# Retention into an ELU feed-forward, one core: the first batch's scores, masks and state copies in another order, output copies written in a row, w_out in 4 KB pieces

## The chip, the cores and the metric

One core of a Trainium2 chip runs the whole kernel. The metric is the device time of one execution in microseconds (us); for the kernel before it is the median of three runs. The engines are PE (TensorE; PEld is its weight load), DVE (VectorE), ACT (ScalarE), POOL (GpSimd) and SP (SyncE), which here only issues transfers. PSUM is the memory that PE writes its products to and that DVE and ACT read; SBUF is the main memory on the core. PSUM is used in banks of 2 KB a partition.

## The reference

Retention without a softmax over 8 batches, 8 heads, 576 positions and 64 values a head, and behind it a feed-forward with ELU:

```python
scores = scale * np.matmul(q, k.transpose(0, 1, 3, 2))         # 8 x 8 x 576 x 576
gamma = 1.0 - 2.0 ** (-5.0 - np.arange(H))                     # one decay a head
Dmat = np.where(rel >= 0, gamma[:, None, None] ** rel, 0.0)    # rel = query position - key position
ret = np.matmul(scores * Dmat, v)                              # 8 x 8 x 576 x 64
x = ret.transpose(0, 2, 1, 3).reshape(4608, 512)
h = x @ w_in                                                   # 512 x 2048
g = np.where(h > 0.0, h, np.exp(np.minimum(h, 0.0)) - 1.0)
out = g @ w_out                                                # 2048 x 512
```

## The kernel before

The decay is folded into queries and keys when they are cast to bf16 (`cast_*`, a product with a small table on DVE or POOL), so scores only need a 0/1 mask. Attention goes by units of 256 positions and 4 heads: a batch has the units (T, w), T the half of 512 positions and w the half of the heads, so units 0 to 3 are batch 0, units 4 to 7 batch 1. (From batch 3 on there are finer units of 128 positions and all heads; the last 64 positions of each batch ride along with other units.)

For each unit the steps are these. Queries and keys are turned on PE and copied from PSUM by ACT or DVE (`turn_q0`, `turn_k0`, `turn_pe`), later by a DMA transpose (`turn`). `scores` writes the products into the one score tile `sc`; `masks` (DVE) multiplies them into `pt` and so frees `sc`. `state` (`states` in the first batch) makes the sums of keys with values. `prefix_mid` and `prefix_end` add them up at the unit's middle and end, on DVE or by an ACT copy, and `put_mid` and `put_end` copy these sums into the tile `s_pair`, on POOL (or into `s_last`, which only the riders of the last 64 positions read). `outputs` takes the two output banks (`new_x`, tiles `x`), does `inter` (queries with the state in `s_pair`) and `values` (`pt` with the values), and `put_x` copies both banks into the bf16 tile `xt`, which the feed-forward reads. A copy of unit 0 to 3 writes elements at steps of four, one of unit 4 to 11 at steps of two, since the positions lie in groups: a partition of q, k or v holds 4 (or 2) positions that lie side by side in memory.

The feed-forward's first product has 16 tiles of 128 features, `ph`: 4 products of 512 columns each (`ffn1`), or for a half of the tokens two tiles of 256 columns (`ffn1_half`). `elu` runs Exp and Relu on ACT and joins them on DVE into `g`. The second product (`ffn2`) adds 16 tiles into `pm`, and ACT copies it out. For group 0, `row(ft)` is the second product's part of one feature tile for two 128-token tiles, and `behind` says after which first-product tile it comes.

Weights come as fp32 through the same staging tiles as q and k (`load_w`, 16 pieces of 512 KB, each in two transfers), and POOL casts most of them (`cast_w`): pieces 0 to 7 are w_in, 8 to 15 w_out. `warm(n)` puts 2n dummy products on PE.

The order on each engine is the order in which the code is written (`pin`, keep_in_program_order). Each engine works through its queue strictly in that order and waits where an input or a buffer isn't ready. Tiles with one tag share a fixed number of buffers: `ph` three banks, `sc` one pair of banks, `x0` and `x1` one bank each, `pt` two, `rv` five.

Of the kernel before, what the change touches and what calls it, by code (L numbers as in the profile page):

```python
# [9 lines left out]
FP32 = mybir.dt.float32  # L10
# [7 lines left out]
def kernel(  # L18
# [9 lines left out]
    nc = tc.nc  # L28
# [35 lines left out]
    def mm(*a, **kw):  # L64
        pin(nc.tensor.matmul(*a, **kw))  # L65
# [97 lines left out]
    staged = {}  # L163

    def weights(k):
        for h in range(2 * (k < 2)):

            r, c = slice(2 * h * P, 2 * (h + 1) * P), slice(k * 2 * P, (k + 1) * 2 * P)
            yield h, moe_w_in[r, c].rearrange("(j p) c -> p j c", j=2), w_in_sb[:, 2 * h : 2 * h + 2, c]
        for i in (2 * k, 2 * k + 1) if k > 1 else ():  # L170
            n, j = divmod(i, KJ)
            if n < KJ:
                c = slice(n * 512, (n + 1) * 512)
                yield i % 2, moe_w_in[j * P : (j + 1) * P, c], w_in_sb[:, j, c]
            else:
                f = i - KJ * KJ
                yield i % 2, moe_w_out[f * P : (f + 1) * P, :], w_out_sb[:, f, :]
# [25 lines left out]

    def load(u, last=False):
        b, T, w = seq[u]
        rqk = raw.tile([P, 2, 4, 2, D], FP32, name="rqk", tag="rqk")
        rv = raw.tile([P, 4, 2, D], FP32, name="rv", tag="rv", bufs=5)
        parts = [(rqk[:, 0], q), (rqk[:, 1], k), (rv, v)]
        if fine(u):
            t = u % 4  # L210
            for dst, src in parts:
                pin(nc.sync.dma_start(
                    dst.rearrange("p a e d -> p (a e) d"), src[b, :, t * P : (t + 1) * P, :].rearrange("h p d -> p h d"),
                ))
            rawt[u] = rqk, rv
            return
        for dst, src in parts[::-1] if last else parts:
# [4 lines left out]
        rawt[u] = rqk, rv  # L222

# [110 lines left out]
    def masks(u, hls=None):  # L334
        sc = score_ps[u]
        if u not in ptt:
            ptt[u] = ppool.tile([P, 2, 2, 2 * P], BF16, name="pt", tag="pt")
            if fine(u):
                ptt[u] = ptt[u].rearrange("p i h n -> p (i h n)")[:, : 2 * HP * C].rearrange("p (i m n) -> p i m n", i=2, m=HP)
# [52 lines left out]
    def put_x(u, hls=(0, 1), to=None, eng="ss"):  # L392
        b, T, w = seq[u]
        h0, h1 = hls[0], hls[-1] + 1
        for c in range(2):
            if fine(u):
                o = w * P + c * C
                pin(engines[eng[c]](xt_tile(b)[:, T, :, o : o + C], xps[c][:, : HP * C].rearrange("p (m n) -> p m n", m=HP)))  # L398
# [4 lines left out]
            pin(engines[eng[c]](dst, src))  # L403
# [246 lines left out]
    def ffn1(g, ft, pool=None, tag="ph", **kw):  # L650

        ph = (pool or ps_h).tile([P, TG], FP32, name="ph", tag=tag)
        for j in range(KJ):
            mm(ph, w_in_sb[:, j, ft * P : (ft + 1) * P], xt_tile(g)[:, :, j], start=(j == 0), stop=(j == KJ - 1))
        gtile(g, ft // 2, 0)
        elu(gts[g, ft // 2][:, :, ft % 2], ph, pairs, **kw)

    def ffn1_half(g, p, hf, **kw):

        ph = ps_h.tile([P, TG], FP32, name="ph", tag="ph")  # L660
        for f in range(2):
            for j in range(KJ):
                mm(ph[:, f * 2 * P : (f + 1) * 2 * P], w_in_sb[:, j, (2 * p + f) * P : (2 * p + f + 1) * P],
                   xt_tile(g)[:, hf, j], start=(j == 0), stop=(j == KJ - 1))
        elu(gtile(g, p, hf).rearrange("p f n -> p (f n)"), ph, **kw)
# [111 lines left out]

    def outputs(u, eng="ss", first=False):
        new_x()
        if first:  # L780
            values(u)
        inter(u)
        if not first:
            values(u)
        put_x(u, eng=eng)
        drop(u)
# [35 lines left out]
    prefix_mid(0, None, "s")  # L822
    turn_k0(1, "s")
    prefix_end(0, None)
# [34 lines left out]
    def part(ft, *js):  # L859
        for j in js:  # L860
            mm(first[ft], w_in_sb[:, j, ft * P : (ft + 1) * P], xt_tile(0)[:, :, j], start=(j == 0), stop=(j == KJ - 1))

    masks(3, (1,))
    cast_w(0, " v")
    inter(3, (0,), banks[0])
    values(3, (0,), banks[0])
    put_x(3, (0,), banks[0])
    part(0, 0)
    part(1, 0)
    inter(3, (1,), banks[1])  # L870
    values(3, (1,), banks[1])
    put_x(3, (1,), banks[1], "sv")
# [40 lines left out]
    load(4)  # L913
    for kk in (14, 15):
        load_w(kk)
    for u in range(5, 10):
        load(u)
    F = {0: {}, 1: dict(pool=ps_h, tag="ph"), 2: dict(pool=ps_h, tag="ph"), 3: {}}
# [26 lines left out]
    cast_w(15)  # L945
    put_end(2)
    put_end(3)
    half1 = f1h(1, 0)
# [11 lines left out]
    cast_v(4, "s")  # L960
    cast(5, "v", "p", None)
    quad(1)
# [9 lines left out]
    quad(3)  # L972
    stretch(5, end=None)
    quad(4)
    turn_pe(6, "vs")
    cast_v(6, "s")
    cast(7, "v", "p", None)
    put_end(5)
    turn(7)
    load(10)  # L980
    quad(5)
# [93 lines left out]
    for hc, (pool, tag, copy, queues) in enumerate((  # L1075
# [4 lines left out]
        for ft in range(NFT):  # L1080
            mm(pm, gtile(B, ft // 2, 1)[:, ft % 2, P:], w_out_sb[:, ft, cols], start=(ft == 0), stop=(ft == NFT - 1))
        ot = opool.tile([P, DM // 2], FP32, name="oe", tag="oe", bufs=2)
        pin(copy(ot, pm))
# [32 lines left out]
```

## Time and profile before

| what | value |
|---|---|
| median of three runs | 303.45 us (303.23 to 303.67) |
| the profiled execution | 304.17 us |
| its span, first to last instruction | 302.2 us |
| PE busy | 290.1 us (96%) |
| DVE, ACT, POOL busy | 176.4, 213.0, 175.1 us |
| granted PE clock | 1.000 |
| read from and written to HBM | 36.70 and 9.44 MB |

Times in rows of the profile count from the span's start. A row of a timeline has start, length, engine, line, operation, output <- input, shapes and count; in brackets stands how long the engine sat idle before it and who ended that. A row of the grouped view ends with busy time, mean ns of one, and the idle time before it. PE's busy time contains 6.57 us of dummy products in the first 10 us, and a record of a product is longer than its share of a dense run, because products overlap.

### The profile page before, as it was taken

The numbers are of one execution on the slowest core, as the hardware profiler recorded it, in microseconds if no ns is written. First come the engines' busy times: TensorE is split into PE (matmuls) and PEld (weight loads), VectorE is DVE, ScalarE is ACT, GpSimd is POOL, SyncE is SP. The second block draws the span as 40 slices with busy tenths as digits, with TensorE's granted clock in tenths as the row PEclk, the third lists the DMA queues.
The fourth block names the chain that finished last, engine by engine and source line by source line (L and its number), as shares of the span: only waits on it lengthen the run. The fifth ranks groups of instructions, "written<-read, shape, count | busy, mean of one in ns | idle before, by whom it ended". The sixth has DMA issues, their size and how long they took to land.

```text
span 302.2 us, 9051 instructions
## 1 busy us (share of the span) xinstructions
PE 290.1 (96%) x3591; PEld 176.5 (58%) x3628; DVE 176.4 (58%) x353; ACT 213.0 (70%) x433; POOL 175.1 (58%) x346
## 2 busy tenths in 40 slices
PE   8789999999999999999999999999999999999995
PEld 5444446776776666666767765554445444456654
DVE  5656568755555666756686765758675734332210
ACT  5679847976767776777777787777777776764531
POOL 7589887687957585868496887468852300011000
PEclk9999999999999999999999999999999999999999
DMA  6999999999999999999799999999761000001112
GB/s 202 316 370 356 346 304 280 227 217 172 248 177 219 169 216 235 206 207 186 191 196 215 184 199 206 202 242 177 172 90 38 37 35 36 37 35 69 37 69 69
DMA packets 132394, 54.33 MB, mean 180 GB/s; under 512 B 107712, under 2 KB 126400, under 8 KB 132352
## 3 DMA queue, kind: packets, MB, share of 16 engines
q1 hardware_dynamic: 129600, 45.04, 74.0%
q0 software_dynamic: 2672, 8.65, 8.6%
q8 instruction: 28, 0.46, 0.7%
q14 instruction: 14, 0.11, 0.1%
q10 hardware_dynamic: 80, 0.07, 0.1%
HBM read 36.70 MB, written 9.44 MB: 153 GB/s over the span
## 4 chain that ended last, share of the span: by engine, by line
PE 89%; DMA 2%; ACT 2%; issue 2%; SPq 1%; POOL 1%; DVE 1%; DVEq 0%; POOLq 0%
PE ph L65 40%; PE pm L65 39%; PE x L65 4%; PE sc L65 3%; DMA rqk<-in_k_dram 2%; PE pe L65 1%; ACT ph L642 1%; POOL s_pair L488 1%; ACT e L639 1%; SPq L731 1%; SPq L717 1%; PE ptr L269 0%; POOL qkn L750 0%; DVE pt L348 0%; DVE pt L354 0%
## 5 line engine op out<-in xcount | busy, mean ns | idle before, releaser
L643 DVE SCALAR_TENSOR_TENSOR g<-e,ph 128x512 bf16<-128x512 f32 x128 | 86.4, 686 | 84.6 <-ACT ph L642 81.2
L65 PE MATMUL ph<-xt,w_in_sb 128*128 128x256 bf16 (+1 forms) x768 | 128.7, 308 | 0.5 <-ACT xt L403 0.3
L65 PE MATMUL pm<-w_out_sb,g 128*128 128x512 bf16 x478 | 123.8, 379 | 3.1 <-issue 2.1
L639 ACT ACTIVATE e<-ph 128x512 f32<-128x512 f32 x144 | 86.0, 597 | 52.8 <-PE ph L65 51.0
L65 PEld LDWEIGHTS <-w_in_sb 128*128 128x128 bf16 x896 | 86.4, 98 | 50.7 <-issue 0.9
L642 ACT ACTIVATE ph<-ph 128x512 f32<-128x512 f32 x144 | 83.8, 591 | 0.0
L65 PEld LDWEIGHTS <-g 128*128 128x128 bf16 x512 | 48.6, 98 | 43.9 <-issue 0.2
L696 POOL DMA_DIRECT2D out_dram<-ot x35 | 19.9, 569 | 44.6 <-ACT ot L686 44.2
L468 POOL CAST s_fine<-run 64x256 bf16<-64x256 f32 x40 | 15.9, 396 | 42.4 <-DVE run L437 33.5
L686 ACT COPY ot<-pm 128x512 f32<-128x512 f32 x35 | 20.5, 588 | 14.9 <-PE pm L65 14.8
L643 DVE SCALAR_TENSOR_TENSOR gt<-e,ph 128x512 bf16<-128x512 f32 x16 | 10.9, 686 | 18.8 <-ACT ph L642 17.2
L227 POOL TENSOR_TENSOR qkn<-rqk,gqf 128x512 bf16<-128x512 f32 x20 | 21.1, 1053 | 0.4
L227 POOL TENSOR_TENSOR qkn<-rqk,gkf 128x512 bf16<-128x512 f32 x20 | 20.9, 1046 | 0.0
L65 PE MATMUL ph<-xtail,w_in_sb 128*128 128x256 bf16 x128 | 16.4, 273 | 0.0
L398 ACT CAST xt<-x 128x256 bf16<-128x256 f32 x40 | 12.9, 378 | 5.0 <-PE x L65 5.0
L437 DVE TENSOR_TENSOR run<-sc,run 128x256 f32<-128x256 f32 x35 | 14.9, 425 | 1.2
L238 POOL CAST vn<-rv 128x512 bf16<-128x512 f32 x24 | 14.6, 608 | 1.5
L341 DVE TENSOR_TENSOR pt<-sc,mask_t 128x512 bf16<-128x512 f32 x20 | 13.7, 684 | 0.0
L488 POOL CAST s_pair<-mid 64x128 bf16<-64x128 f32 x24 | 7.0, 292 | 11.4 <-DVE mid L437 6.6
L474 POOL CAST s_fine<-run 64x256 bf16<-64x256 f32 x30 | 11.9, 395 | 1.8
L459 DVE COPY qs<-qkT 64x256 bf16<-64x256 bf16 x40 | 12.0, 300 | 0.6
L65 PE MATMUL sc<-qkT 64*64 64x64 bf16 (+1 forms) x512 | 11.6, 204 | 0.5 <-ACT qkT L760 0.4
(106 smaller groups left out, 270.2 us busy)
## 6 DMA issues: line engine op xcount, KB each, us to landing
rqk<-in_q_dram SPq DMA_DIRECT2D x32, 256.0 KB, 4.3
rqk<-in_k_dram SPq DMA_DIRECT2D x32, 256.0 KB, 5.4
rv<-in_v_dram SPq DMA_DIRECT2D x32, 256.0 KB, 5.5
out_dram<-ot POOLq DMA_DIRECT2D x31, 256.0 KB, 3.4
rqk<-in_moe_w_in_dram SPq DMA_DIRECT2D x16, 256.0 KB, 5.7
rqk<-in_moe_w_out_dram SPq DMA_DIRECT2D x16, 256.0 KB, 5.9
rqt<-in_q_dram SPq DMA_DIRECT2D x8, 128.0 KB, 5.2
rqt<-in_k_dram SPq DMA_DIRECT2D x8, 128.0 KB, 4.5
```

The costliest lines, as they stand in the source:

```text
L65: pin(nc.tensor.matmul(*a, **kw))
L227: pin(tt[eng](natt[u][0][:, i].rearrange("p e h d -> p (e h) d"), rawt[u][0][:, i].rearrange("p a e d -> p (a e) d"), (gqf, gkf)[i][:, u % ...
L238: pin(engines[eng](natt[u][1], rawt[u][1]))
L341: pin(nc.vector.tensor_tensor(ptt[u], sc[:, :, : HP * C].rearrange("p i (m n) -> p i m n", m=HP), mask_t.unsqueeze(1).unsqueeze(1).to_broa ...
L398: pin(engines[eng[c]](xt_tile(b)[:, T, :, o : o + C], xps[c][:, : HP * C].rearrange("p (m n) -> p m n", m=HP)))
L437: pin(nc.vector.tensor_tensor(dst, a, b, ALU.add))
L468: pin(nc.gpsimd.tensor_copy(s_fine[u % 2][half(1), :, i], new[half(i), 0]))
L639: pin(nc.scalar.activation(e, ph, AF.Exp))
L642: pin(nc.scalar.activation(ph, ph, AF.Relu))
L643: pin(nc.vector.scalar_tensor_tensor(dst, view(e), -1.0, view(ph), ALU.add, ALU.min))
L686: pin(nc.scalar.copy(ot, pm))
L696: pin((queue or nc.gpsimd).dma_start(dst, src))
```

## The change

- The first batch is written in another order. Scores and mask of unit 2 come ahead of the outputs of unit 0; the outputs of unit 1 go to two banks of the `ph` tag (tiles `y`) in place of the `x` banks, behind the scores of unit 3; the state copies keep their order but for unit 1's end, which moves ahead. Unit 1's key copy goes from ACT to DVE, and unit 3's value cast from POOL to ACT. `pt` has three buffers. For unit 3, `values` comes ahead of `inter`.
- `put_x` walks its elements in the order of the output, so that it writes in a row and reads PSUM in steps of 32 (units 0 to 3) or 64 elements (units 4 to 11).
- The two feature tiles of a pair are interleaved: a tile takes every second column of w_in, and w_out's rows 2p and 2p+1 go to partition p. Seven of the eight w_out pieces come so in one transfer of 512 KB with 4 KB pieces; the eighth keeps two.
- `row(ft)` follows its first-product tile at a distance of four for all tiles; before it was three up to tile 10.
- The end states of units 2 and 3 are copied by ACT, a little later, and unit 5's queries are cast by POOL instead of DVE. The values of unit 9 are loaded behind the transpose of unit 7. The last tile's output uses the `ot` buffers.

The core of the diff:

```diff
+    def features(ft):
+        return slice(ft // 2 * 2 * P + ft % 2, (ft // 2 + 1) * 2 * P, 2)
@@ load_w
+        if k > KJ * KJ // 2:
+            n = k - KJ * KJ // 2
+            pin(nc.sync.dma_start(
+                staged[k].rearrange("p e c -> p (e c)"),
+                moe_w_out[2 * n * P : 2 * (n + 1) * P, :].rearrange("(p e) c -> p (e c)", e=2),
+            ))
+            return
@@ put_x
-            src = (to or xps)[c][:, : 2 * P].rearrange("p (h e r) -> p h e r", h=2, e=e)[:, h0:h1]
-            dst = xt_tile(b)[:, T, 2 * w + h0 : 2 * w + h1, c * P : (c + 1) * P].rearrange("p h (r e) -> p h e r", e=e)
+            src = (to or xps)[c][:, : 2 * P].rearrange("p (h e r) -> p h r e", h=2, e=e)[:, h0:h1]
+            dst = xt_tile(b)[:, T, 2 * w + h0 : 2 * w + h1, c * P : (c + 1) * P].rearrange("p h (r e) -> p h r e", e=e)
@@ ffn1, ffn1_half, part
-            mm(ph, w_in_sb[:, j, ft * P : (ft + 1) * P], xt_tile(g)[:, :, j], ...)
+            mm(ph, w_in_sb[:, j, features(ft)], xt_tile(g)[:, :, j], ...)
@@ first batch
-    turn_k0(1, "s")
+    turn_k0(1, "v")
...
     prefix_mid(1, None, "s")
+    cast_k0(3, "p", (0,))
+    scores(2, 1)
+    cast_v0(3, "s")
+    cast_k0(3, "v", (1,))
+    prefix_end(1, None)
+    masks(2)
+    put_mid(1)
+    turn_k0(3, "s")
     outputs(0)
-    cast_k0(3, "p", (0,))
-    prefix_end(1, None)
-    cast_k0(3, "v", (1,))
-    put_mid(1)
     put_end(0)
-    cast_v0(3, "p")
-    scores(2, 1)
-    masks(2)
-    turn_k0(3, "s")
-    outputs(1)
+    put_end(1)
     st2 = states(2)
     prefix_mid(2)
     prefix_end(2, None)
-    put_end(1)
     scores(3, 1)
+    ys = [ps_h.tile([P, TG], FP32, name="y", tag="ph") for _ in range(2)]
+    outputs(1, ys)
+    st3 = states(3)
     cast_w(0, "s ")
-    st3 = states(3)
-    outputs(2, first=True)
+    outputs(2)
+    masks(3, (0,))
     prefix_mid(3)
-    masks(3, (0,))
@@ feed-forward of group 0
-    behind = {4: (0, 1), 11: ()}
-    behind.update({ft: (ft - (3 if ft < 11 else 4),) for ft in range(5, 16) if ft != 11})
+    behind = {4: (0, 1), 5: ()}
+    behind.update({ft: (ft - 4,) for ft in range(6, 16)})
@@ units 4 to 9
-    put_end(2)
-    put_end(3)
...
-    cast(5, "v", "p", None)
+    put_end(2, "s")
+    put_end(3, "s")
+    cast(5, "p", "p", None)
...
     turn(7)
+    load(9, "v")
     load(10)
```

ACT's queue in the first batch, before. `qkT<-ptr` is a turned copy of queries or keys, `mid<-st` a state sum, `vn<-rv` a value cast, `xt<-x` the output copies:

```order
L760 COPY qkT<-ptr 128x512 x2
L448 COPY mid<-st 128x128
L760 COPY qkT<-ptr 128x512
L238 COPY vn<-rv 128x512 x2
L760 COPY qkT<-ptr 128x512
L448 COPY mid<-st 128x128
L403 COPY xt<-x 128x2x4x32 x2
L760 COPY qkT<-ptr 128x512
L403 COPY xt<-x 128x2x4x32 x2
L187 COPY w_in_sb<-rqk 128x2x256
L403 COPY xt<-x 128x2x4x32 x2
```

The same place in the changed kernel, whose line numbers are higher by 11 or 12:

```order
L772 COPY qkT<-ptr 128x512 x2
L460 COPY mid<-st 128x128
L249 COPY vn<-rv 128x512 x2
L772 COPY qkT<-ptr 128x512
L460 COPY mid<-st 128x128
L249 COPY vn<-rv 128x512
L772 COPY qkT<-ptr 128x512
L415 COPY xt<-x 128x2x128 x2
L415 COPY xt<-y 128x2x128 x2
L198 COPY w_in_sb<-rqk 128x2x256
L415 COPY xt<-x 128x2x128 x2
```

Unit 1's key copy is gone, unit 3's value cast has come in, and unit 3's key copy stands ahead of the first output copies. The outputs of unit 1 come from `y`.

POOL's queue there, before: half of unit 3's key cast, state copies (`s_pair`, from middle and end sums), unit 3's value cast and the first w_in casts:

```order
L750 TENSOR_TENSOR qkn<-rqk,gk 128x256
L488 COPY s_pair<-mid 64x2x64 x2
L488 COPY s_pair<-end 64x2x64 x2
L238 COPY vn<-rv 128x512
L488 COPY s_pair<-mid 64x2x64 x2
L488 COPY s_pair<-end 64x2x64 x2
L488 COPY s_pair<-mid 64x2x64 x2
L187 COPY w_in_sb<-rqk 128x2x256 x2
```

And after:

```order
L762 TENSOR_TENSOR qkn<-rqk,gk 128x256
L500 COPY s_pair<-mid 64x2x64 x2
L500 COPY s_pair<-end 64x2x64 x4
L500 COPY s_pair<-mid 64x2x64 x4
L198 COPY w_in_sb<-rqk 128x2x256 x2
```

The value cast has left the queue, and the end state of unit 1 is ahead of the middle state of unit 2.

More of the change, by code (lines that the diff above doesn't have):

```diff
@@ L202, with load @@
     xps, begun = [None, None], set()
-    def load(u, last=False):
+    def load(u, what="qkv"):
         b, T, w = seq[u]
-        rqk = raw.tile([P, 2, 4, 2, D], FP32, name="rqk", tag="rqk")
-        rv = raw.tile([P, 4, 2, D], FP32, name="rv", tag="rv", bufs=5)
-        parts = [(rqk[:, 0], q), (rqk[:, 1], k), (rv, v)]
+        if u not in rawt:
+            rawt[u] = (raw.tile([P, 2, 4, 2, D], FP32, name="rqk", tag="rqk"),
+                       raw.tile([P, 4, 2, D], FP32, name="rv", tag="rv", bufs=5))
+        rqk, rv = rawt[u]
+        parts = [{"q": (rqk[:, 0], q), "k": (rqk[:, 1], k), "v": (rv, v)}[x] for x in what]
         if fine(u):
@@ L214, in load @@
                 ))
-            rawt[u] = rqk, rv
             return
-        for dst, src in parts[::-1] if last else parts:
+        for dst, src in parts:
             pin(nc.sync.dma_start(
@@ L221, in load @@
             ))
-        rawt[u] = rqk, rv
     def cast_qk(u, i, eng, es=(0, 1)):
@@ L336, in masks @@
         if u not in ptt:
-            ptt[u] = ppool.tile([P, 2, 2, 2 * P], BF16, name="pt", tag="pt")
+            ptt[u] = ppool.tile([P, 2, 2, 2 * P], BF16, name="pt", tag="pt", bufs=3)
             if fine(u):
@@ L653, in ffn1 @@
         for j in range(KJ):
-            mm(ph, w_in_sb[:, j, ft * P : (ft + 1) * P], xt_tile(g)[:, :, j], start=(j == 0), stop=(j == KJ - 1))
+            mm(ph, w_in_sb[:, j, features(ft)], xt_tile(g)[:, :, j], start=(j == 0), stop=(j == KJ - 1))
         gtile(g, ft // 2, 0)
@@ L662, in ffn1_half @@
             for j in range(KJ):
-                mm(ph[:, f * 2 * P : (f + 1) * 2 * P], w_in_sb[:, j, (2 * p + f) * P : (2 * p + f + 1) * P],
+                mm(ph[:, f * 2 * P : (f + 1) * 2 * P], w_in_sb[:, j, features(2 * p + f)],
                    xt_tile(g)[:, hf, j], start=(j == 0), stop=(j == KJ - 1))
@@ L776, in states, with outputs @@
         return st
[L778 to L785, printed above, removed]
+    def outputs(u, to=None):
+        if to is None:
+            new_x()
+        inter(u, to=to)
+        values(u, to=to)
+        put_x(u, to=to)
         drop(u)
@@ L860, in part @@
         for j in js:
-            mm(first[ft], w_in_sb[:, j, ft * P : (ft + 1) * P], xt_tile(0)[:, :, j], start=(j == 0), stop=(j == KJ - 1))
+            mm(first[ft], w_in_sb[:, j, features(ft)], xt_tile(0)[:, :, j], start=(j == 0), stop=(j == KJ - 1))
     masks(3, (1,))
     cast_w(0, " v")
+    values(3, (0,), banks[0])
     inter(3, (0,), banks[0])
-    values(3, (0,), banks[0])
     put_x(3, (0,), banks[0])
@@ L869 @@
     part(1, 0)
+    values(3, (1,), banks[1])
     inter(3, (1,), banks[1])
-    values(3, (1,), banks[1])
     put_x(3, (1,), banks[1], "sv")
@@ L913 @@
     load(4)
[L914 to L917, printed above, removed]
+    load_w(14)
+    load_w(15)
+    load(5)
+    load(6)
+    load(7)
+    load(8)
+    load(9, "qk")
     F = {0: {}, 1: dict(pool=ps_h, tag="ph"), 2: dict(pool=ps_h, tag="ph"), 3: {}}
@@ L972 @@
     quad(3)
-    stretch(5, end=None)
+    stretch(5, "p", end=None)
     quad(4)
@@ L977 @@
     cast(7, "v", "p", None)
-    put_end(5)
+    put_end(5, "p")
     turn(7)
+    load(9, "v")
     load(10)
@@ L1081 @@
             mm(pm, gtile(B, ft // 2, 1)[:, ft % 2, P:], w_out_sb[:, ft, cols], start=(ft == 0), stop=(ft == NFT - 1))
-        ot = opool.tile([P, DM // 2], FP32, name="oe", tag="oe", bufs=2)
+        ot = opool.tile([P, DM], FP32, name="ot", tag="ot")[:, : DM // 2]
         pin(copy(ot, pm))
```

2 lines of the change are left out of this document (1 added, 1 removed).

## The prediction

> **What bounds the kernel now.** I read the page's first part, then a table of stretches, then the timelines of PE, ACT, DVE and POOL in the one stretch where PE is not full.
>
> ```profile
> PE 290.1 (96%) x3591; PEld 176.5 (58%) x3628; DVE 176.4 (58%) x353; ACT 213.0 (70%) x433; POOL 175.1 (58%) x346
> ...
> 10.00:20.88 10.88, 7.97 (x198) 5.04 (x199) 6.69 (x13) 8.47 (x17) 8.04 (x20) 1.00 1.09 343
> 20.88:39.20 18.32, 18.20 (x91) 8.13 (x86) 10.19 (x16) 16.23 (x31) 16.53 (x29) 1.00 1.05 354
> 39.20:52.00 12.80, 12.43 (x199) 7.57 (x201) 10.41 (x20) 7.78 (x16) 9.91 (x22) 1.00 1.10 288
> 52.00:290.00 238.00, 234.79 (x2983) 145.10 (x3012) 141.36 (x275) 172.90 (x353) 134.86 (x252) 1.00 0.83 157
> ```
>
> The stretch rows give length, then busy time of PE, PEld, DVE, ACT and POOL, granted clock (1.00), DMA share and GB/s. From 20.88 us to 290 PE idles 0.12, 0.37 and 3.21 us in 269. From 10.00 to 20.88 it idles 2.91 us in 10.88, in the first batch's attention. So a change can win there, a microsecond or so, and later it can mostly only lose. PE's timeline of that stretch (start, length, what; in brackets the wait before it):
>
> ```profile
> 12.33 0.42 PE L65 MATMUL sc<-qkT 64*64 64x128 bf16 x16 [0.39 <-ACT qkT L760]
> 13.95 0.28 PE L65 MATMUL x<-qkT,s_pair 128*128 128x128 bf16 x2 [0.29 <-POOL s_pair L488]
> 14.84 0.42 PE L65 MATMUL sc<-qkT 64*64 64x128 bf16 x16
> 15.98 0.27 PE L65 MATMUL x<-qkT,s_pair 128*128 128x128 bf16 x2 [0.39 <-POOL s_pair L488]
> ...
> 16.98 0.42 PE L65 MATMUL sc<-qkT 64*64 64x128 bf16 x16
> ...
> 17.98 0.41 PE L65 MATMUL x<-pt,vn 64*64 64x128 bf16 x14 [0.33 <-ACT xt L403]
> ...
> 19.23 0.23 PE L65 MATMUL st<-qkT,s_pair 128*128 128x128 bf16 x1 [0.45 <-POOL s_pair L488]
> 20.01 0.59 PE L65 MATMUL ph<-xt,w_in_sb 128*128 128x512 bf16 x2 [0.31 <-ACT xt L403]
> ```
>
> The waits are for ACT's copies and POOL's state copies, in turn: a chain through four engines. Its last link, the start of the first feed-forward product at 20.01, is where I measure the gain, since PE is dense soon after.
>
> **The first batch's order.** The other engines in that stretch:
>
> ```profile
> 13.70 0.58 ACT L760 COPY qkT<-ptr 128x512 bf16<-128x512 bf16 x1 [0.16 <-PE ptr L759]
> 14.18 0.27 ACT L448 COPY mid<-st 128x128 f32<-128x128 f32 x1
> 14.62 1.31 ACT L403 CAST xt<-x 128x256 bf16<-128x256 f32 x2 [0.17 <-PE x L65]
> ...
> 17.67 0.69 ACT L187 CAST w_in_sb<-rqk 128x512 bf16<-128x512 f32 x1
> 18.65 1.31 ACT L403 CAST xt<-x 128x256 bf16<-128x256 f32 x2 [0.29 <-PE x L65]
> ...
> 7.46 0.42 DVE L760 COPY qkT<-ptr 128x512 bf16<-128x512 bf16 x1 [0.38 <-PE ptr L759]
> 12.80 1.22 DVE L348 TENSOR_TENSOR pt<-sc,mask_q 128x1024 bf16<-128x1024 f32 x1 [0.69 <-PE sc L65]
> 15.31 1.22 DVE L348 TENSOR_TENSOR pt<-sc,mask_q 128x1024 bf16<-128x1024 f32 x1 [0.20 <-PE sc L65]
> ...
> 12.13 1.18 POOL L750 TENSOR_TENSOR qkn<-rqk,gk 128x256 bf16<-128x256 f32 x2 [1.59 <-DMA rqk<-in_k_dram]
> 15.32 0.62 POOL L488 CAST s_pair<-end 64x128 bf16<-64x128 f32 x2
> 16.01 0.61 POOL L238 CAST vn<-rv 128x512 bf16<-128x512 f32 x1
> 18.55 0.62 POOL L488 CAST s_pair<-mid 64x128 bf16<-64x128 f32 x2
> ```
>
> I follow the new order with these durations, allowing about 0.05 us for each hand-over between engines.
>
> Unit 1's keys: their turned copy goes to DVE, 0.42 us instead of ACT's 0.58, and no longer stands behind ACT's state copy. Scores 1 start near 12.0 instead of 12.33, and their mask ends near 13.7 instead of 14.02.
>
> Unit 2: its keys' copy on ACT ends at 13.70 + 0.58 = 14.28 either way, since POOL's cast at 12.13 waited for a DMA. Before, outputs 0 stood between; now scores 2 follow at 14.3 (was 14.84). Mask 2 starts 0.47 later, as at 12.33 to 12.80: 14.8 to 16.0 (was 15.31 to 16.53). Scores 3, behind a dummy pair that needs the mask's end, start near 16.4 (was 16.98, 0.45 behind the mask's end at 16.53).
>
> ACT now has a value cast (0.63) behind its state copy: 14.45 to 15.15. Unit 3's key copy runs to 15.75 and the pair of output copies of unit 0 behind it. Queued behind that value cast are thus the key copy and outputs 0; nobody needs either before scores 3 at 16.4 and outputs 2 near 17.3, because unit 1 has its own banks now and needn't wait for unit 0's. That is the step that replaces the wait before 15.98.
>
> PE does outputs 1 behind scores 3, ready near 17.15. ACT then does pair 1, the cast of w_in (0.6 net) and pair 2, whose input is ready near 17.95.
>
> POOL loses the 0.61 us cast between its state copies: the first state of unit 1 is placed by 16.55, unit 2's middle by 17.2. The last, of unit 3, now waits for DVE's sum (near 17.8) and ends near 18.5 instead of 18.55 + 0.62 = 19.17. The wait at 19.23 ends near 18.55.
>
> **What a pair of output copies costs** decides the rest. Now the copies read PSUM in a row and write in steps; afterwards they read in steps and write in a row. No row of before reads PSUM in steps. The nearest:
>
> ```profile
> 47.45 0.77 ACT L403 CAST xt<-x 128x256 bf16<-128x256 f32 x2
> 101.50 0.65 ACT L398 CAST xt<-x 128x256 bf16<-128x256 f32 x2
> ```
>
> The pair at 14.62 writes 2-byte elements at steps of 8 bytes and takes 1.31; the pair at 47.45, at steps of 4 bytes, 0.77; the pair at 101.50 writes in a row, 0.65. Output step alone doubled the price. If reads in steps are free the pair costs 0.65; if they cost as much as such writes, about 1.3; both sides of a penalty of that size again, 2.0. I take 0.65, since that row has the new output pattern, and keep 0.65 to 2.0; below 0.65 nothing speaks for it.
>
> The Trainium skill (SBUF — State Buffer, Door 1) says 8-byte steps of bf16 are still free, two hits in a 16-byte line being enough; this trace disagrees (1.31 against 0.65). The same place gives PSUM lines of 8 bytes and says that stepped access is slow there for matmuls; no run here shows it for ACT's reads. By it the first rival below would happen.
>
> With 0.65: pair 1 17.15 to 17.8, w_in to 18.4, pair 2 to 19.05, the first product at 19.1 instead of 20.01. **Gain 0.9 us.** The work of PE behind it is the same as before, and unit 3's two halves, whose copies lose their steps too, arrive as far ahead of their readers as now.
>
> **The other edits.** *Strided w_in weights*: 896 weight loads now take every second column. No row shows such a load.
>
> ```profile
> L65 PEld LDWEIGHTS <-w_in_sb 128*128 128x128 bf16 x896 | 86.4, 98 | 50.7 <-issue 0.9 <-DVE xt L403 0.3
> ...
> 45.12 0.61 PE L269 MATMUL ptr<-ident,qkn 128*128 128x128 bf16 x8
> 45.57 1.03 PE L65 MATMUL pm<-w_out_sb,g 128*128 128x512 bf16 x4
> ...
> 51.29 2.78 PE L65 MATMUL ph<-xt,w_in_sb 128*128 128x256 bf16 x24
> L65 PE MATMUL ph<-xt,w_in_sb 128*128 128x256 bf16 x512 | 65.4, 273 | 0.2 <-DVE g L643 0.2
> L65 PE MATMUL ph<-xtail,w_in_sb 128*128 128x256 bf16 x128 | 16.4, 273 | 0.0
> ```
>
> A load is recorded at 98 ns, but eight turns, each with its own load, go from 45.12 to the next product at 45.57, (45.57 - 45.12) / 8 = 56 ns apiece, so a load holds the path for 56 ns at most. A 256-column product takes (2.78 - 0.27) / 23 = 109 ns (0.27 is the last one's own length), and covers it; a load could be 53 ns longer at no cost. Nothing, then, from this row; beyond 53 ns each further ns costs 640 x 1 ns = 0.64 us. The Trainium skill (TensorE: Matmul & The Clock Gate, Weight-path perf modes) lets the fast load keep its form for column steps up to 1,024 elements; no run here shows it, and by it the price is nothing too.
>
> *Rows of the second product one step later, w_out in 512 KB transfers*: the same products in another order. POOL's casts follow the DMA there:
>
> ```profile
> 32.36 0.61 POOL L187 CAST w_in_sb<-rqk 128x512 bf16<-128x512 f32 x1 [0.65 <-DMA rqk<-in_moe_w_in_dram]
> ...
> 36.10 1.18 POOL L235 TENSOR_TENSOR qkn<-rqk,gq 128x256 bf16<-128x256 f32 x2 [0.31 <-DMA rqk<-in_q_dram]
> ...
> 39.56 2.04 POOL L187 CAST w_out_sb<-rqk 128x512 bf16<-128x512 f32 x3 [0.57 <-DMA rqk<-in_moe_w_out_dram]
> 41.54 1.67 POOL L492 CAST s_last<-end 64x128 bf16<-64x128 f32 x4
> ...
> 33.58 1.89 PE L65 MATMUL ph<-xt,w_in_sb 128*128 128x512 bf16 x8
> 43.23 1.90 PE L65 MATMUL pm<-w_out_sb,g 128*128 128x512 bf16 x7
> ...
> 44.95 1.07 ACT L686 COPY ot<-pm 128x512 f32<-128x512 f32 x2 [2.71 <-PE pm L65]
> ```
>
> PE needs the w_in piece cast until 32.97 for tile 12, the second four of the eight products at 33.58, so at about 34.4, and w_out's last row, cast until 41.6, at the end of the run from 43.23, about 44.6: slack 1.4 and 3.0 us, of which the earlier start uses 0.9. A joined transfer brings its first 256 KB only with its second, some 0.74 us later at the stretch's 354 GB/s; the slack of 0.5 to 2.1 left covers that nearly. Price 0, at worst 0.4.
>
> *Unit 5's queries to POOL, state copies of units 2 and 3 (1.67 us) from POOL to ACT*: POOL gains 1.67 and gives 1.18; ACT waits from 42.24 to 44.95 for PE in that place (the wait of 2.71 in its row), and four copies of 0.27, the state copy's price at 14.18, fit. *Values of unit 9 behind a transpose in SP's queue, the last tile from another pool, later output copies at 0.65 instead of 0.77*: beside full PE, 0.
>
> **Sum.** The profiled execution took 304.17 us with a span of 302.2, so 302.2 - 0.9 = 301.3 and 303.27. The median of the runs is 303.45, so I forecast **302.55**; 0.6 to 1.5 us of gain, as hand-overs fall, is 301.95 to 302.85.
>
> **Rivals.** *Stepped PSUM reads are slow.* ACT's chain is 17.15 + pair + 0.6 + pair; it breaks even with 19.96, where pair 2 ends now, at 1.1 a pair. At 1.3 pair 2 ends at 20.35: 0.4 slower, 303.85. At 2.0 pair 0 ends only at 17.75 and pair 2 at 22.35: 2.4 slower, **305.85**. For it: the step in the output doubled the price. Against: the step is on another memory, and fp32.
>
> *The start is earlier, but the stretch to 52 us gives it back.* POOL's three waits for DMA in the rows above show a loaded stream that an earlier PE doesn't hasten; where the joined transfers come later than I think, 0.4 to 0.9 returns as waits of PE near 33 to 45 us: 302.95 to **303.45**. Against: pieces of 4 KB in place of 2 should not come later.
>
> *Weight loads lengthen.* If a strided load doubles from 98 to 196 ns, 45 ns over the margin, 640 x 45 ns = 28.8 us comes on top: **331**. Against: the margin, for which a load must nearly double.
>
> **How the numbers follow.** Forecast 0.64; slow reads 0.17 (0.07 near 1.3 a pair, 0.10 well above); gain given back 0.13; weight loads 0.06. A difference of 0.2%, 0.6 us, is about what a measurement of this kernel tells from none: faster 0.64, same 0.13 + 0.07 = 0.20, slower 0.10 + 0.06 = 0.16. The range goes from 301.7 to 304.1: outside it lie those 0.16 and some 0.03 below.
>
> **What would show it.** First product near 19.1; scores 1, 2 and 3 at 12.0, 14.3 and 16.4; a pair of output copies at 0.65 (a pair over 1.1 makes me wrong, and PE then waits for xt before the first product); no wait on POOL before 18.5; 256-column products still at 109 ns apart (otherwise the third rival); PE's idle time from 20.88 to 52 still near 0.5 us (otherwise the second).

## The result, and the profile after

The changed kernel takes 303.00 us, median of 22 runs, beside 303.86 us for the kernel before, also 22 runs: a ratio of 0.9968 [0.9958, 0.9979]. That is 0.86 us faster; forecast were 0.9 us and 302.55, inside a range of 301.7 to 304.1. The span is 301.2 us (before 302.2).

The page's first line and the same four stretches, in the same columns:

```profile
PE 292.7 (97%) x3628; PEld 176.1 (58%) x3628; DVE 175.9 (58%) x352; ACT 211.4 (70%) x437; POOL 174.4 (58%) x343
10.00:20.88 10.88, 9.10 (x205) 5.40 (x205) 7.59 (x17) 7.03 (x20) 7.89 (x21) 1.00 1.09 344
20.88:39.20 18.32, 18.30 (x86) 8.23 (x84) 10.31 (x15) 16.65 (x32) 15.66 (x28) 1.00 1.04 367
39.20:52.00 12.80, 12.80 (x207) 8.02 (x205) 9.07 (x17) 8.48 (x21) 10.17 (x24) 1.00 1.09 271
52.00:290.00 238.00, 237.59 (x3009) 144.68 (x3007) 141.48 (x275) 172.97 (x354) 134.40 (x248) 1.00 0.83 156
```

From 10.00 to 20.88 us PE idles 1.78 us where it idled 2.91. The stretches behind need care: this trace has all 3628 product records, as many as weight loads, and that of before had 3591. A missing record looks like idle time, so much of the 0.37 and 3.21 us that the prediction counted there as waits of PE was never a wait. Here they are 0 and 0.41.

PE's timeline of the first batch, after:

```profile
11.65 0.42 PE L65 MATMUL sc<-qkT 64*64 64x128 bf16 x16
13.96 0.42 PE L65 MATMUL sc<-qkT 64*64 64x128 bf16 x16 [0.19 <-ACT qkT L772]
15.71 0.38 PE L65 MATMUL sc<-zero 128*128 128x256 bf16 x2 [0.34 <-DVE pt L359]
16.02 0.42 PE L65 MATMUL sc<-qkT 64*64 64x128 bf16 x16
18.42 0.23 PE L65 MATMUL st<-qkT,s_pair 128*128 128x128 bf16 x1 [0.31 <-POOL s_pair L500]
18.80 0.59 PE L65 MATMUL ph<-xt,w_in_sb 128*128 128x512 bf16 x2 [0.16 <-ACT xt L415]
```

ACT's and POOL's there:

```profile
15.31 0.65 ACT L415 CAST xt<-x 128x256 bf16<-128x256 f32 x2
17.04 0.65 ACT L415 CAST xt<-y 128x256 bf16<-128x256 f32 x2 [1.08 <-PE y L65]
17.57 0.63 ACT L198 CAST w_in_sb<-rqk 128x512 bf16<-128x512 f32 x1
18.09 0.66 ACT L415 CAST xt<-x 128x256 bf16<-128x256 f32 x2
11.76 1.19 POOL L762 TENSOR_TENSOR qkn<-rqk,gk 128x256 bf16<-128x256 f32 x2 [1.61 <-DMA rqk<-in_k_dram]
17.72 0.64 POOL L500 CAST s_pair<-mid 64x128 bf16<-64x128 f32 x2 [0.74 <-DVE mid L449]
```

A pair of output copies takes 0.65 us instead of 1.31, and the first product starts at 18.80 instead of 20.01. But the 1.21 us between is not all the change's. The chain of waits shows where the start hangs. Before (start, length, what; these pieces of it):

```profile
5.00 7.00 DMA rqk<-in_k_dram
...
13.98 0.61 POOL qkn L750
14.59 0.24 POOL s_pair L488
...
19.13 0.83 ACT xt L403
```

And after:

```profile
5.57 6.06 DMA rqk<-in_k_dram
...
14.44 1.24 DVE pt L359
...
15.71 0.73 PE sc L65 x18
16.44 0.62 PE y L65 x18
...
18.09 0.67 ACT xt L415 x2
```

Both begin with the transfer of unit 2's keys; POOL's cast of them follows, at 12.13 before and at 11.76 after. The change leaves the order of the transfers up to there as it was, and in the 13 traces with this order, all profiled kernels but one, that cast starts anywhere between 11.01 and 12.39 us. So I measure from it: 20.01 - 12.13 = 7.88 us to the first product before, 18.80 - 11.76 = 7.04 after. **0.84 us is the change, 0.37 the landing.** (The five traces with the old first batch lie at 11.50 to 12.39, the eight with the new one at 11.01 to 12.04. So the traces alone don't exclude that the change moves the landing a little; the times, 0.86 us beside 0.84, leave little room for it.) The chain's middle differs as meant: before it runs through POOL's queue of state copies, after through scores, masks and output copies.

### The profile page after: what moved, and what is told of

It is laid out like the page before. It is cut to its first block, busy times and chain, and to the rows that moved or that the text cites. A ratio compares the mean times of both kernels' runs of the same rounds, so it can differ in the third digit from the quotient of the medians.

```text
span 301.2 us, 9084 instructions
## 1 busy us (share of the span) xinstructions
PE 292.7 (97%) x3628; PEld 176.1 (58%) x3628; DVE 175.9 (58%) x352; ACT 211.4 (70%) x437; POOL 174.4 (58%) x343
## 4 chain that ended last, share of the span: by engine, by line
PE 91%; ACT 3%; DMA 2%; SPq 1%; DVE 1%; issue 1%; POOL 0%; ACTq 0%; POOLq 0%
PE pm L65 40%; PE ph L65 40%; PE x L65 4%; PE sc L65 3%; DMA rqk<-in_k_dram 2%; PE pe L65 1%; SPq L743 1%; DVE pt L359 1%; ACT ph L654 1%; ACT e L651 1%; SPq L729 1%; ACT xt L415 1%; PE ptr L280 0%; POOL qkn L762 0%; PE y L65 0%
## 5 line engine op out<-in xcount | busy, mean ns | idle before, releaser
L65 PE MATMUL pm<-w_out_sb,g 128*128 128x512 bf16 x512 | 129.6, 379 | 0.0
```

## The experiments

Two distances carry the reading of each trace: d1 from the start of POOL's cast of unit 2's keys to the first product, and d2 from there to the first product of 256 columns, 50.22 us in the changed kernel; d2 tells whether the stretch in between gives a gain back. Behind that point all kernels with this w_in layout or the old one need 250.8 to 251.2 us to the end.

| kernel | median us | ratio to before | d1 | d2 |
|---|---|---|---|---|
| before | 303.86 | 1 | 7.88 | 31.28 |
| weights' part alone | 303.97 | 1.0000 [0.9983, 1.0017] | 7.87 | 31.37 |
| copies in a row alone | 303.63 | 0.9986 [0.9960, 1.0011] | 7.11 | 31.90 |
| copies and unit 5's work | 303.09 | 0.9969 [0.9950, 0.9989] | 7.12 | 31.93 |
| copies and weights' part | 303.07 | 0.9991 [0.9967, 1.0014] | 7.14 | 31.31 |
| changed | 303.00 | 0.9968 [0.9958, 0.9979] | 7.04 | 31.42 |
| changed, again | 302.88 | 0.9968 [0.9955, 0.9980] | 7.04 | 31.70 |
| changed, old copies | 304.77 | 1.0034 [1.0015, 1.0054] | 8.26 | 31.55 |
| changed, unit 5's work as before | 303.03 | 0.9966 [0.9944, 0.9988] | 7.04 | 31.32 |
| changed, without the weights' part | 303.07 | 0.9983 [0.9959, 1.0007] | 7.04 | 31.41 |

The kernels were compared in three groups, each with its own runs of before (303.86 to 303.90, 303.85 and 303.74 us). The intervals are about as wide as the effects; where times don't separate two kernels, d1 and d2 of one execution each do, and only the traces are then the evidence, one execution for each kernel. The recorded ratio isn't the quotient of the medians, and a few long executions pull it: for copies and weights' part the medians, 303.07 and 303.74, would give 0.9978, but two of its twelve executions ran at a granted clock of 0.992 and 0.982 and took 304.34 and 306.60 us. Without the weights' part three of twelve ran at 0.989 to 0.994 and took 304.2 to 305.8.

### The order with the old copies

The changed kernel, with `put_x` walking its elements as before:

```diff
-            src = (to or xps)[c]...rearrange("p (h e r) -> p h r e", h=2, e=e)[:, h0:h1]
+            src = (to or xps)[c]...rearrange("p (h e r) -> p h e r", h=2, e=e)[:, h0:h1]
```

> The changed kernel with one thing undone: put_x walks the elements in the old order, so the output copies write in steps again. Theory (copies and order together set the first batch's chain): a pair of output copies takes 1.31 us again instead of 0.65; unit 1's pair can start at 17.04 as now, then 17.04 + 1.31, the cast of w_in 0.6 and the next pair 1.31 end near 20.2, so the first feed-forward product starts near 20.2 instead of 18.80 and the time is 1.2 to 1.4 us over the changed kernel's, 0.2 to 0.4 over that of before. Rival (the order alone brings the gain, since ACT has time to spare ahead of unit 1's outputs): within 0.3 us of the changed kernel.

PE's first product, and ACT's copies, of this kernel:

```profile
20.30 0.59 PE L65 MATMUL ph<-xt,w_in_sb 128*128 128x512 bf16 x2 [1.26 <-ACT xt L415]
17.31 1.32 ACT L415 CAST xt<-y 128x256 bf16<-128x256 f32 x2 [0.40 <-PE y L65]
18.37 0.68 ACT L198 CAST w_in_sb<-rqk 128x512 bf16<-128x512 f32 x1
18.95 1.30 ACT L415 CAST xt<-x 128x256 bf16<-128x256 f32 x2
```

PE waits 1.26 us for ACT, whose two slow pairs now stand one behind the other with only the w_in cast between. d1 is 8.26: the new order alone makes the start 0.38 us later, and the kernel slower than before. The start is the one expected; the time isn't, 0.87 us over its runs of before (303.90) in place of 0.2 to 0.4. Six of its twelve executions had a granted clock of 0.988 to 0.994 and took 305.0 to 306.2 us; the other six have a median of 304.1, that is 0.4 over the 303.7 of those 29 of the 35 runs of before whose clock was 0.997 or more. Everything else is the changed kernel, so this also measures the copies inside it: 8.26 - 7.04 = 1.22 us at the first product.

### The copies alone, and with one other part each

The kernel before, with the output copies in a row; then the same with unit 5's work, and the same with the weights' part (columns, 4 KB pieces, rows one step later):

```diff
-            src = (to or xps)[c]...rearrange("p (h e r) -> p h e r", h=2, e=e)[:, h0:h1]
+            src = (to or xps)[c]...rearrange("p (h e r) -> p h r e", h=2, e=e)[:, h0:h1]
```

> The kernel before with only the output copies changed: they write in a row and read PSUM in steps. Theory: pairs at 0.65 us, but in the old order the first product still waits behind the state copy of unit 3 on POOL, which ends at 19.17 whatever ACT does; first product near 19.5 instead of 20.01, 0.3 to 0.6 us faster than before. Rival (the copies alone bring all of the gain): 0.9 to 1.1 us faster. Rival (the order alone): within 0.2 us of before.

```diff
-    put_end(2)
-    put_end(3)
...
-    cast(5, "v", "p", None)
+    put_end(2, "s")
+    put_end(3, "s")
+    cast(5, "p", "p", None)
```

> The kernel before, with output copies that write in a row, and with unit 5's queries on POOL and the placing of the states of units 2 and 3 on ACT. Theory A: the 0.77 us that the copies alone won at the first product are kept up to 52 us, since DVE's mask of unit 4 no longer stands behind a cast that waits for a DMA: 0.6 to 0.8 us faster than before, a ratio of 0.9974 to 0.9980. Rival B: the wait at unit 5's turn comes from the landing of its keys or from elsewhere and stays: a ratio near 0.9986 as with the copies alone.

> The kernel before, with two parts of the change: output copies that write in a row, and the weights' part (strided w_in columns, w_out in 4 KB pieces, its rows one step later); the order of the first batch and unit 5's work stay as before. Theory A (with the copies alone the 0.77 us won at the first product was given back because the stream of weights lands too late for it, and the weights' part is what makes it land earlier): PE waits for nothing from 19.5 to 52 us, the first half-product stands 31.3 to 31.5 us behind the first product instead of 31.9, and the time is 0.7 to 0.9 us below before, a ratio of 0.9970 to 0.9978, as the whole change. Rival B (it was the order of unit 5's work): a wait of 0.3 to 0.6 us near unit 5's turn at 45 us remains, a ratio near 0.9986.

d1 falls to 7.11, 7.12 and 7.14: the copies alone bring 0.77 of the 0.84 us. With nothing else they lose most of it again before 52 us, 0.62 us by d2. Of the copies alone, POOL's cast of unit 2's keys and its last state copy, PE behind that copy, at the first product and at unit 5's turn, then DVE ahead of that turn:

```profile
12.39 1.18 POOL L750 TENSOR_TENSOR qkn<-rqk,gk 128x256 bf16<-128x256 f32 x2 [1.60 <-DMA rqk<-in_k_dram]
18.43 0.62 POOL L488 CAST s_pair<-mid 64x128 bf16<-64x128 f32 x2
19.11 0.23 PE L65 MATMUL st<-qkT,s_pair 128*128 128x128 bf16 x1 [0.45 <-POOL s_pair L488]
19.50 0.60 PE L65 MATMUL ph<-xt,w_in_sb 128*128 128x512 bf16 x2
45.23 0.61 PE L269 MATMUL ptr<-ident,qkn 128*128 128x128 bf16 x8 [0.59 <-DVE end L437]
42.57 0.86 DVE L235 TENSOR_TENSOR qkn<-rqk,gq 128x256 bf16<-128x256 f32 x2 [1.52 <-DMA rqk<-in_q_dram]
43.34 1.21 DVE L348 TENSOR_TENSOR pt<-sc,mask 128x1024 bf16<-128x1024 f32 x1
```

As the first expectation had it, the start now ends in POOL's last state copy, 19.05 - 12.39 = 6.66 us behind the key cast. That the first product stands at the expected 19.50 is partly luck, since the keys landed 0.26 us later than in the kernel before. Later DVE waits 1.52 us for the transfer of unit 5's queries; behind the waiting cast stands the mask of unit 4, and behind that the state sum for which PE waits 0.59 us. The chain of waits of this kernel, from 12.30 us on, is a chain of transfers:

```profile
12.30 6.21 DMA rqk<-in_moe_w_in_dram
...
18.52 5.86 DMA rqk<-in_moe_w_out_dram
...
35.38 7.16 DMA rqk<-in_q_dram
```

So the stream of weights had become the bound. With unit 5's work moved, the wait at the turn is gone, as theory A of its expectation has it, but that execution waited at another place of the stream (PE's row, and the chain's):

```profile
28.67 0.59 PE L65 MATMUL pm<-w_out_sb,g 128*128 128x512 bf16 x2 [0.34 <-POOL w_out_sb L187]
21.43 6.51 DMA rqk<-in_moe_w_out_dram
```

So d2 stays at 31.93. The times, 303.09 us and a ratio of 0.9969, say theory A; the trace says that the gain was lost, and one execution can't settle which of the two is the rule.

With the weights' part, no wait over 0.2 us lies between the first product, 18.85, and 50.16, and d2 is 31.31: theory A of its expectation, by the trace. Its ratio doesn't show it, the interval holds both theories and no gain; the medians differ by 0.67 us.

### The weights' part, alone and left out

> The kernel before with only the weights' edits: every second column of w_in in a tile, w_out in 4 KB pieces, rows of the second product one tile later. Theory: PE is dense there and its weight loads have 53 ns to spare, so within 0.2 us of before. Rival (the transfers bring the gain): 0.5 to 1.0 us faster. Rival (strided loads cost something that the order wins back): slower by 0.3 us or more.

303.97 us, ratio 1.0000: nothing. With the late start the stream is early enough, d2 is 31.37 beside 31.28. And the changed kernel without it:

> The changed kernel without the weights' part: w_in columns side by side, w_out in 2 KB pieces, its rows as early as before. Theory A: the last piece of w_out lands about 41.5 us instead of 40, PE waits 0.3 to 0.6 us in all for w_out near 28 us or for unit 5's queries and keys near 44 us, and 0.3 to 0.6 us of the gain go: a ratio of 0.9980 to 0.9990. Rival B (price nothing, as predicted): the ratio of the whole change, 0.9960 to 0.9970.

d1 7.04, d2 31.41, a span of 300.9 us: no wait returns, although the last w_out piece landed at 40.4 us as against 39.8. So rival B holds by the trace; the ratio, 0.9983 [0.9959, 1.0007], settles nothing.

### Unit 5's work put back

```diff
+    put_end(2)
+    put_end(3)
...
-    put_end(2, "s")
-    put_end(3, "s")
-    cast(5, "p", "p", None)
+    cast(5, "v", "p", None)
```

> The changed kernel, with the work of unit 5 put back as before: the placing of the states of units 2 and 3 on POOL, right behind the casts of the last w_out pieces, and unit 5's queries cast on DVE again. Theory A (this edit, which the prediction priced at nothing, is what keeps the start's gain): the first product stands where it does in the changed kernel, but DVE's cast of unit 5's queries waits for its DMA ahead of unit 4's mask and POOL's cast of its keys comes some 0.5 to 1 us later than the 42.16 of the changed kernel, so unit 5's turn waits 0.3 to 0.6 us for POOL or DVE: 0.3 to 0.6 us slower than the changed kernel, a ratio to before of 0.9980 to 0.9990. Rival B (the price is nothing, as predicted): no wait at that turn, the time of the changed kernel, a ratio of 0.9960 to 0.9970.

Rival B holds: the time is the changed kernel's. Its DVE, and PE's scores of unit 4:

```profile
40.39 0.97 DVE L246 TENSOR_TENSOR qkn<-rqk,gq 128x256 bf16<-128x256 f32 x2 [0.71 <-DMA rqk<-in_q_dram]
41.37 1.23 DVE L359 TENSOR_TENSOR pt<-sc,mask 128x1024 bf16<-128x1024 f32 x1
40.90 0.42 PE L65 MATMUL sc<-qkT 64*64 64x128 bf16 x16
```

DVE again waits for the queries ahead of the mask, but they land early enough: the cast ends at 41.36, the scores at 41.32. So my theory that this edit keeps the gain was wrong. By these traces either of two things is enough, the weights' part or the new order with unit 5's work; in the two kernels that have neither, the stream takes most of the gain back. The new order without both the weights' part and unit 5's work was not run.

### The changed kernel once more

> The changed kernel once more, for a second profile on the same chip as the others. Theory: 0.9 to 1.1 us faster than before; the DMA that unit 2's keys wait for may land some tenths of a us earlier or later than at 11.76, and the first scores move with it, without changing the distance from there to the first product (7.0 us in the first profile, 7.9 before). Rival (the early DMA of the first profile is a part of the change): it lands within 0.1 us of 11.76 again.

303.90 - 302.88 = 1.02 us faster, as expected. The cast of unit 2's keys starts at 11.80, so within 0.1 us of 11.76, as the rival has it; but in the four later traces with the same start it stands at 11.01, 11.08, 11.45 and 11.49, so that place belongs to the execution. d1 is 7.04 to the hundredth again, as in all six executions of that start. d2 is 0.28 longer, and most of that comes at one place, where POOL and PE have these rows:

```profile
28.54 2.45 POOL L198 CAST w_out_sb<-rqk 128x512 bf16<-128x512 f32 x4 [0.64 <-DMA rqk<-in_moe_w_out_dram]
29.21 0.59 PE L65 MATMUL pm<-w_out_sb,g 128*128 128x512 bf16 x2
```

The first of POOL's four casts, which waited for its transfer, ends near 28.54 + 0.61 = 29.15, and PE's row of the second product follows at 29.21, 10.37 us behind the first product. In the first profile of the changed kernel that cast starts at 27.96 and the row stands at 28.93, 10.13 behind. So the stream of weights can bind in the changed kernel too, for 0.24 us here.

### Can the start be shortened further?

Both edits of the first kernel, and the second of them alone:

```diff
-            load_kv0(w, what)         # order k0 v0 k1 v1 k2 v2 ...
+    ...                               # order k0 v0 k1 k2 v1 v2 ...
-    scores(2, 1)
+    scores(2)
-    scores(3, 1)
+    scores(3)
```

> The changed kernel with two further edits at the start: unit 2's keys are loaded ahead of unit 1's values, and scores 2 and 3 go without the pair of zero products ahead of them, which needs the end of the mask before. Theory A (the start's chain runs through the landing of unit 2's keys at 11.8 us and through the zero products' wait of 0.3 us): POOL's cast of unit 2's keys starts 0.3 to 0.6 us earlier, scores 3 start up to 0.4 us earlier, the first product near 18.3 to 18.5 instead of 18.8, and the time is 0.3 to 0.7 us below that of the changed kernel, 302.2 to 302.6 us. Rival B (the start's bound is elsewhere, ACT's two pairs of copies and the w_in cast between them, or unit 1's values, now later): the first product stays within 0.1 us of 18.8 and the time within 0.3 us of 302.9; a granted clock lower at the start, for want of the zero products, would show in products longer than 0.42 a score.

> The changed kernel, where scores 2 and 3 go without the pair of zero products ahead of them. Theory A (the chain from the landing of unit 2's keys to the first product, 7.04 us in four executions of the changed order, runs through the zero products, which wait 0.3 us for the end of mask 2 and take 0.3 more): 6.6 to 6.8 us, so 0.25 to 0.45 us earlier, and a time 0.2 to 0.4 us below the changed kernel, 302.5 to 302.8 us. Rival B (ACT's chain of pair 1, w_in and pair 2 ends last anyway): 7.0 us, same time.

Neither gains beyond the noise: 303.02 us, ratio 0.9970 [0.9949, 0.9990], and 303.27, 0.9983 [0.9967, 1.0000]. With the earlier keys POOL's cast starts at 10.81, and the first product at 18.37. That is inside theory A's 18.3 to 18.5, but no gain: kernels without these edits started theirs at 18.05 to 18.84, as their keys landed, and from the cast it is 7.56 us. The chain of waits then begins with unit 3's keys, which landed at 13.4, and runs through POOL's state copies. Without the zero products d1 grows to 7.51. Two stretches (columns as above) and PE's scores 3 and first product of that kernel:

```profile
14.00:16.00 2.00, 1.93 (x63) 1.52 (x56) 1.80 (x4) 1.75 (x4) 1.73 (x7) 0.66 1.09 361
16.00:18.00 2.00, 2.00 (x57) 1.55 (x58) 1.52 (x4) 1.03 (x3) 0.89 (x4) 0.50 1.06 385
15.40 0.64 PE L65 MATMUL sc<-qkT 64*64 64x128 bf16 x16
18.96 0.59 PE L65 MATMUL ph<-xt,w_in_sb 128*128 128x512 bf16 x2 [0.35 <-ACT xt L415]
```

Scores 3 start 0.31 us sooner behind the key cast (15.40 - 11.45 = 3.95 against 4.26), as theory A has it, and then take 0.64 us instead of 0.42: the granted clock is 0.66 and 0.50 there. The zero products buy the clock here. The Trainium skill (TensorE: Matmul & The Clock Gate, Part 1) has the clock fall to half after an idle window of PE, one that runs freely; the 0.50 agrees, though PE was not quite idle ahead of it, 0.92 us busy in the 2.00 from 12 to 14. In the profiled execution of the kernel with both edits the clock stayed at 1.00. How often it falls can be read from the granted clock of every execution: it was 0.994 or lower in 9 of the 12 without the zero products and in 6 of the 12 with both edits, but in only 4 of the 46 of the four kernels with the changed start that were measured beside these two. The profiled execution above, with its one stretch at 0.50, had 0.994.

### What a stepped weight load costs

The changed kernel, with w_in columns at larger steps; in the second kernel each step has its own line (L66 step 4, L67 8, L68 16, L69 32, L70 64):

```diff
-            mm(ph, w_in_sb[:, j, features(ft)], xt_tile(g)[:, :, j], ...)
+            mm(ph, w_in_sb[:, j, ft:DF:16] if g else w_in_sb[:, j, features(ft)], xt_tile(g)[:, :, j], ...)
```

> The changed kernel, where the first feed-forward product of all batches but the first takes its w_in columns at a step of 16 elements (32 bytes) instead of 2, so that the output of those batches is not the reference's; the number, shape and order of the instructions stay. Theory A: a weight load costs the same at any step, 98 ns recorded and 109 ns from one 256-column product to the next, and the time is that of the changed kernel, 302.9 us. Rival B: a load that takes one element from each 32 bytes is slower; a load that doubles to 196 ns is about 45 ns over what a 256-column product hides and costs 640 x 45 ns = 28.8 us; the pace shows it even if it is only a few ns over the margin of 53.

> The changed kernel, where the first feed-forward product takes its w_in columns at a step of 4 elements in batch 1, 8 in batch 2, 16 in 7 and 8, 32 in 3 and 5, 64 in 4 and 6, so that these outputs are not the reference's; each step has a line of its own in the profile. With step 16 a load was recorded at 141 to 143 ns instead of 98 and cost nothing. Theory A (a load lengthens with the step up to the 32 bytes that step 16 spans, then no more): 98 ns at 4, about 100 to 120 at 8, 143 at 16, 32 and 64, all hidden by the 256-column product's 109 ns and its 53 ns of margin, and the time of the changed kernel, 302.9 us. Theory B (it lengthens further, by 45 ns with each doubling): 190 ns at 32 and 235 at 64, so over the margin by 39 and 84 ns on the 128 products of 256 columns each of batches 3 and 4: 128 x 39 + 128 x 84 ns = 16 us slower, with 256-column products 148 and 193 ns apart.

Grouped weight loads, first of the changed kernel (step 2), then with step 16 (128 of the 896 loads are of batch 0 at step 2), then the mixed steps; the second number behind the bar is the mean ns of one:

```profile
L65 PEld LDWEIGHTS <-w_in_sb 128*128 128x128 bf16 x896 | 86.5, 98 | 50.4 <-issue 0.9 <-POOL w_in_sb L198 0.3
```

```profile
L65 PEld LDWEIGHTS <-w_in_sb 128*128 128x128 bf16 x896 | 107.6, 141 | 34.8 <-issue 1.0
```

```profile
L70 PEld LDWEIGHTS <-w_in_sb 128*128 128x128 bf16 x192 | 26.6, 173 | 5.6
L68 PEld LDWEIGHTS <-w_in_sb 128*128 128x128 bf16 x192 | 24.1, 144 | 7.5
L69 PEld LDWEIGHTS <-w_in_sb 128*128 128x128 bf16 x192 | 23.9, 144 | 7.7
L67 PEld LDWEIGHTS <-w_in_sb 128*128 128x128 bf16 x128 | 14.9, 144 | 2.8
L66 PEld LDWEIGHTS <-w_in_sb 128*128 128x128 bf16 x128 | 13.7, 114 | 2.2 <-issue 0.3
```

98 ns at step 2, as side by side; 114 at 4; 144 at 8, 16 and 32; 173 at 64. Neither theory had that curve (A said 98 at 4 and 144 at most, B 190 and 235). A of step 16, the load unchanged at 98, was wrong as well; what held was that 28.8 us, or 16, didn't come. PE at step 64:

```profile
144.28 1.04 PE L70 MATMUL ph<-xt,w_in_sb 128*128 128x256 bf16 x8
```

That is (1.04 - 0.27) / 7 = 110 ns from one product to the next, where the prediction had 109 for the old layout; by the starts of the records the median is 109 or 110 at every step. Behind 50 us both kernels need 251.6 and 251.7 us, 0.6 us more than the changed kernel, so a longer load isn't quite free. The times: 303.40 us, ratio 0.9975 [0.9954, 0.9996], and 303.72, 1.0002 [0.9984, 1.0021].

## Why the prediction was right, point by point

- **The size and its place.** 0.9 us at the first product was forecast; d1 shows 0.84, the times 0.86. Two misses inside the sum nearly cancel. Pair 1 was to start at 17.15; it started at 17.04, or 17.41 with the 0.37 of the earlier landing added, 0.26 late. From there to the end of pair 2 it took 18.75 - 17.04 = 1.71 us and not 19.05 - 17.15 = 1.90. The forecast lay 0.45 us under the median because its base did: the three runs of before gave 303.45, the 22 gave 303.86.
- **Pair of copies, 1.31 to 0.65.** Exactly so (378 ns the median copy). Reading PSUM at steps of 32 fp32 elements costs ACT nothing; writing 2-byte elements at steps of 8 bytes had doubled the price. The first rival, slow stepped reads, is refuted; the slow stepped access to PSUM that the Trainium skill (SBUF — State Buffer, Door 1) gives for matmuls does not hold for these reads.
- **The break-even at 1.1 us a pair.** With 1.3 a pair the prediction had pair 2 end at 20.35, that is 8.22 behind the key cast at 12.13; with the old copies in the new order it ended at 18.95 + 1.30 = 20.25, 8.21 behind its cast at 12.04.
- **Scores at 12.0, 14.3 and 16.4.** Measured 11.65, 13.96 and 16.02; with the 0.37 of the earlier landing added, 12.02, 14.33 and 16.39. (Scores 1 hang on an earlier transfer; the turn ahead of them stands at 10.21 instead of 10.60, so it moved about as much.)
- **What the moved steps bring.** This term was mis-sized. The prediction worked out the gain step by step along the new order, with the copies' price as its condition, and never priced the copies in the old order. The copies alone brought 0.77 us, the order on top of them 0.07 to 0.10. With equal landings (11.77 and 11.76) scores 3 start 0.51 us sooner with the new order (16.53 against 16.02), but the outputs of unit 1, moved behind them, take 0.62 us of the chain (16.44 to 17.06) and hand that back.
- **POOL's last state copy.** Forecast to end at 18.5, so 6.4 behind the key cast; it ended at 17.72 + 0.64 = 18.36, 6.6 behind. PE's 0.31 us for it lie ahead of a wait for ACT, which ends last. The forecast gave the earlier end to the value cast that left POOL's queue. But with the copies alone, and that cast still there, the copy ended 6.66 behind, against 7.04 before; in the new order POOL waits 0.74 us for DVE's sum at that place.
- **Weight loads at nothing.** Right at step 2: 98 ns, 109 ns apart. The margin of 53 ns was sound, loads longer by 46 (144 ns) stayed hidden; at 173 ns, over the margin by 22, the 2.8 us that it implied for the 128 products of batch 4 at step 64 didn't come: 53 ns was a lower bound, as worked out. Either the true margin is at least 75, or a longer record of a load doesn't hold the path for as much longer; the runs don't tell these apart.
- **Weights' part, unit 5's work at nothing.** Right in the sum, each alone also; but not free of each other. The second rival, a stretch to 52 us that gives the gain back, is real: it is what the copies alone ran into, with the bound that the rival named, a stream that an earlier PE doesn't hasten. The prediction gave that a chance of 0.13 without saying that the change holds two guards against it.
- **PE idle near 0.5 us from 20.88 to 52.** 0.02; the 0.5 was mostly missing records.

Open: how much of the 0.9 us that the old copies cost in the times, against 0.65 by d1 and d2 together (39.81 against 39.16), is the lower clock of half of their executions; in how many executions PE waits for the w_out piece near 29 us, 0.34 us with unit 5's work and 0.24 in the changed kernel's second profile; and why the new order lets the stream come early enough without the weights' part.

## What to carry to other kernels

When a copy between two memories must step on one side, try it on each side: here the cost was all in the narrow writes, none in the wide reads. Before you book a gain at one place, look at what arrives next there, and measure from the event on which the chain hangs, not from the span's start, since a transfer's landing can move by as much as the change. An edit that measures nothing alone may be what keeps another's gain, so try pairs before you call it idle.

## What the runs showed of the hardware that was not expected

A weight load of 128 bf16 columns lengthens with the column step: 98 ns up to 2 elements, 114 at 4, 144 from 8 to 32, 173 at 64. The Trainium skill (TensorE: Matmul & The Clock Gate, Weight-path perf modes) gives steps up to 1,024 elements as the range of the fast load and no price by step; the runs show one.

Two pairs of zero products, 0.6 us of PE in all (0.31 from the start of the second pair to the scores behind it), decided about the clock: with them it was 1.00 in the traces of the changed start, without them 0.50 from 16 to 18 us in one of two. And the landing of one transfer early in the kernel, with the same order of transfers ahead of it, varied by 1.4 us over 13 traces, of 12 kernels and one repeat.
